# A routed slot's split weights kept in one buffer and remade in a branch where the expert changes

## The chip, the cores and the metric

One Trainium2 chip, one core. The metric is the device time of one execution in microseconds: 819.39 us, the median of three runs (816.16 to 824.21).

## The reference, cut to what matters

Three stages follow each other: a gated recurrent attention, a mixture of experts that sends each token to one of eight, and a feed-forward layer with a cosine in it. The change lies in the second stage and in what the third finds when it begins.

```python
def _moe_ref(x, modality_id, w_gate, modality_bias, w1, w2):   # x 3072x320, w1 8x320x1024, w2 8x1024x320
    logits = x @ w_gate + modality_bias[modality_id]
    e_idx = np.argmax(logits, axis=1)
    ...
    for e in range(E):
        mask = e_idx == e
        h = np.maximum(x[mask] @ w1[e], 0.0)
        out[mask] = gate_w[mask, None] * (h @ w2[e])
    return out

def _moe2_ref(x, w_in, w_out):                                  # w_in 320x2048, w_out 2048x320
    h = x @ w_in
    g = h * np.cos(h)
    return g @ w_out
```

## The kernel before

The tokens of each expert are gathered into slots of 256 rows (`SLOT`). There are twelve such slots (`NS`), in the order of their experts, and up to seven short ones of 128 rows for what is left over (`shorts`). Which expert a slot has is worked out on the chip: `tab0` and `tab` hold each slot's expert and a flag that says whether it differs from that of the slot ahead. `load_w` reads both into registers of SP and issues the loads of the raw weights under the flag: `w1r` and `w2r`, in two halves.

Matmuls run on a split of each operand in two `fp32r` parts, so raw weights must be split before they are used. `split` does it for one f, one of the eight 128-wide pieces of the hidden dimension (`NF`): ACT copies the high parts (`WIH`, line 906, and `WOH`, line 909), and DVE or POOL subtract them from the raw values (line 898, in `sub`): `WIL` and the last rows of `WIH`, and `WOL`. The split weights have two buffers, and slot s uses number s % 2. `prep(n)` makes the split for step n = 8 s + f some steps ahead, for each slot anew, whether the raw weights have changed or not. By the table `VP`, DVE takes the `WIL` part always and the two others at f = 3 and 4; POOL takes the two others at the six other f.

A step of a slot (`bstep(s, f)`, slots 2 to 11) is, in program order: `ffn1` (eight matmuls, line 935), `relu` (ACT line 941, then DVE line 942, into `hh` and `hl`), `ffn2` two steps behind (six matmuls, line 956; its last two steps run in the next slot's f = 0 and 1), one `prep`, and one step of `_decode`. That generator turns the third stage's weights, which lie in memory as 64-bit floats, into 32-bit ones on DVE (lines 1690 to 1707): pieces 3 to 19, each of 5 steps with 6 instructions, loaded by SP into two buffers `raw`. At f = 0 the next slot's rows are gathered (POOL line 828) and `load_w` of the next slot's first half stands; its second half stands at f = 4. At f = 4 to 6 the next slot's rows are transposed and split (`xpose_b`: PE line 848, ACT line 852, DVE line 853). `finish` writes a slot's result (ACT line 971, POOL lines 972 and 962). Every engine works through its own instructions in program order, so DVE's part of a `relu` waits for whatever stands ahead of it on DVE.

Slots 0 and 1 have a loop of their own (line 1306, steps k = 0 to 15), in which DVE also works out the order of the other slots, a chain of small instructions (`plan`, `halves`, `slot_index`, `slot_table`, `out_rows`). There, `prep` is given to POOL altogether for the steps 4 to 9.

The third stage's weights need the same split (`split_c`, sixteen pieces): six pieces stand in slot 11, two in the short slots, and eight in the first tile of the third stage (`c_ffn1`, `c_phase`, `c_cos`, `c_split`, `c_ffn2`). A branch on all engines (line 1540) jumps over the short slots that are not there.

Of the kernel before, what the change touches and what calls it, by code (L numbers as in the profile page):

```python
# [23 lines left out]
DM = H * D  # L24
# [69 lines left out]
def kernel(  # L94
# [816 lines left out]

    VP = ((), (3, 4))

    def prep(n, eng=V):
        s, f = divmod(n, NF)
        if s < NS:
            split(w1r, w2r, f, (s % 2) * NF + f, eng, V if f in VP[bool(s)] else G_)

# [6 lines left out]
    def ffn1(s, f):  # L925
        fs = slice(f * 128, (f + 1) * 128)
        xh, xl = (t_[:, :, (s % 2) * SLOT:(s % 2 + 1) * SLOT] for t_ in (XH, XL))
        ph = hbank(s, f)
        W, Wl = WIH[s % 2][:, :, fs], WIL[s % 2][:, :, fs]
        mms = (  # L930
            (W[:, 0], xh[:, 0]), (Wl[:, 0], xh[:, 0]), (W[:, 1], xh[:, 1]), (Wl[:, 1], xh[:, 1]), (W[:, 2], xh[:, 2]),
            (W[:, 0], xl[:, 0]), (W[:, 1], xl[:, 1]), (W[:, 2], xl[:, 2]),
        )
        for n, (a, x_) in enumerate(mms):
            T_.matmul(out=ph, lhsT=a, rhs=x_, start=(n == 0), stop=(n == len(mms) - 1))  # L935
# [60 lines left out]
    dec, xgs = [iter(())], {}  # L996

# [308 lines left out]
    for k in range(2 * NF):  # L1306
        s, f = divmod(k, NF)
        ffn1(s, f)
        if k == 7:
# [8 lines left out]
        if k == 11:  # L1318
# [191 lines left out]
    qw.close()  # L1510
    qu = ExitStack()
    qu_ = pool(qu, "qu")
    w1u = qu_.tile([128, 3, DF1], F32, name="w1u")
    w2u = qu_.tile([128, NF, DM], F32, name="w2u")
    for a in range(2):
        wu_t[a] += [qu_.tile([128, DM], F32R, name=f"wu{a}{i}") for i in range(2, 4)]
    load_u(1, 0)
    load_u(1, 1)
    xg = xpose_c(0, XS, XH, XL, (2, 3, 2))

    def extra0():
        split_c(6)
        yield
        split_c(7)
        yield
        next(xg)
        yield
        next(xg)
        yield
        next(xg)  # L1530
        yield
# [8 lines left out]
    with ExitStack() as tail:  # L1540
        for u in range(2, NU):
# [89 lines left out]
    for n in range(len(seq) + LAG - 2):  # L1631
# [152 lines left out]
```

## Time and profile before

| | us |
|---|---|
| median of three runs (lowest, highest) | 819.39 (816.16, 824.21) |
| the profiled execution, its own time | 826.95 |
| its span, first to last instruction | 825.2 |
| busy: PE, DVE, ACT, POOL | 735.9, 637.7, 438.3, 340.1 |
| mean granted TensorE clock | 0.947 |

The profile comes from one execution, and its trace is read through views. [...] The timeline gives start, duration, engine, line and operation. The view of groups gives for one kind of instruction the busy time, the mean of one, and how long its engine sat idle just before it. The waits view names who was waited for. L898 is line 898 of the kernel. A duration in the trace can overlap the next instruction's, so the step from one start to the next is what an engine needs for one instruction.

### The profile page before, as it was taken

The page shows a single profiled execution, that of the slowest core. Times are in us where ns is not written, and L with a number is a line of the kernel's source. Part 1 is how long each engine was busy: PE and PEld are TensorE (multiplying, and loading weights), DVE is VectorE, ACT ScalarE, POOL GpSimd, SP SyncE. Part 2 cuts the span into 40 slices and gives each one's busy share as a digit, 9 for nine tenths or more (in the row PEclk, how much of TensorE's full clock was granted, in tenths as well). Part 3 has the DMA queues.
Part 4 walks back from the last instruction along what each step waited for, and adds up shares of the span by engine and source line. Part 5 has one row for each costly group of instructions (what it writes and reads, how often), then busy time and mean ns, then how long its engine had stood idle before and what let it go on. Part 6 is the DMA issues. An engine that isn't in the chain of part 4 may idle for free. (4 is left out here: it accounts for less than half of the span.)

```text
span 825.2 us, 16649 instructions
## 1 busy us (share of the span) xinstructions
PE 735.9 (89%) x5947; PEld 671.1 (81%) x5948; DVE 637.7 (77%) x1320; ACT 438.3 (53%) x1039; POOL 340.1 (41%) x450
## 2 busy tenths in 40 slices
PE   9878988867898889988968899999999999999995
PEld 6777777756887888988858689989899998999995
DVE  6877787779769998999988598767676776666762
ACT  4545555444455555655646466555555555555552
POOL 7646564455587787877875330200200200100201
PEclk6999899989989999989989999999999999999998
DMA  7798787831132282332463201001001000000000
GB/s 180 200 211 226 214 238 219 248 119 41 50 101 62 80 228 70 106 92 68 146 201 105 67 1 33 33 0 33 33 1 33 33 1 1 33 1 0 33 2 33
DMA packets 48650, 73.71 MB, mean 89 GB/s; under 512 B 5518, under 2 KB 33776, under 8 KB 48560
## 3 DMA queue, kind: packets, MB, share of 16 engines
q1 hardware_dynamic: 43808, 59.01, 25.8%
q0 software_dynamic: 3648, 11.82, 4.4%
q10 hardware_dynamic: 1104, 1.75, 0.7%
q8 instruction: 49, 0.80, 0.4%
q14 instruction: 41, 0.34, 0.2%
HBM read 89.82 MB, written 12.22 MB: 124 GB/s over the span
## 5 line engine op out<-in xcount | busy, mean ns | idle before, releaser
L1596 ACT ACTIVATE w1r<-w1r 128x512 f32<-128x512 f32 x96 | 60.7, 632 | 104.2 <-DVE w1r L1591 104.2
L1598 DVE TENSOR_TENSOR w1r<-bk,w1r 128x512 f32<-128x512 f32 x96 | 66.2, 690 | 50.5 <-ACT w1r L1596 49.0
L1589 ACT ACTIVATE w1r<-bk,qtr 128x512 f32<-128x512 f32 x96 | 65.9, 686 | 55.7 <-PE bk L1584 55.7
L935 PE MATMUL bk<-XH,WIH 128*128 128x256 f32 x288 | 81.7, 309 | 15.2 <-POOL WIH L898 5.3
L1590 DVE TENSOR_SCALAR w1r<-w1r 128x512 f32<-128x512 f32 x96 | 41.1, 428 | 51.1 <-ACT w1r L1589 51.0
L941 ACT ACTIVATE hh<-bk 128x256 fp32r<-128x256 f32 x96 | 36.7, 382 | 75.5 <-PE bk L935 75.4
L898 DVE TENSOR_TENSOR WIL<-w1r,WIH 128x256 fp32r<-128x256 f32 x88 | 68.9, 784 | 8.8 <-ACT WIH L906 8.7
L1591 DVE TENSOR_TENSOR w1r<-w1r 128x512 f32<-128x512 f32 x96 | 70.6, 736 | 3.3
L935 PEld LDWEIGHTS bk<-XH,WIH 128*128 128x128 f32 x288 | 58.1, 202 | 18.4 <-POOL WIH L898 6.7
L956 PE MATMUL bk<-WOH,hl 128*128 128x320 f32 x192 | 62.8, 327 | 9.6 <-DVE hl L942 9.6
L1616 PE MATMUL bk<-WOH,gh 128*128 128x320 f32 x228 | 71.0, 312 | 0.0
L1616 PE MATMUL bk<-WOH,gl 128*128 128x320 f32 x228 | 70.6, 310 | 0.0
L1616 PE MATMUL bk<-WOL,gh 128*128 128x320 f32 x228 | 70.5, 309 | 0.0
L898 POOL TENSOR_TENSOR WOL<-w2r,WOH 128x320 fp32r<-128x320 f32 x74 | 67.2, 908 | 0.7 <-ACT WOH L909 0.7
L956 PE MATMUL bk<-WOH,hh 128*128 128x320 f32 x192 | 63.0, 328 | 0.0
L1584 PE MATMUL bk<-XH,WIH 128*128 128x512 f32 x144 | 57.8, 402 | 5.3 <-PEq L1540 4.0
L956 PE MATMUL bk<-WOL,hh 128*128 128x320 f32 x192 | 62.4, 325 | 0.0
L935 PE MATMUL bk<-XL,WIH 128*128 128x256 f32 x288 | 54.6, 298 | 4.5 <-DVE XL L853 4.5
L1584 PE MATMUL bk<-XL,WIH 128*128 128x512 f32 x144 | 57.3, 398 | 0.0
L1584 PE MATMUL bk<-xh,WIH 128*128 128x512 f32 x144 | 56.5, 393 | 0.0
L1584 PE MATMUL bk<-xl,WIH 128*128 128x512 f32 x144 | 56.1, 390 | 0.0
L906 ACT ACTIVATE WIH<-w1r 128x384 fp32r<-128x384 f32 x96 | 49.9, 519 | 9.5 <-DMA w1r<-in_w_dram 9.5
(382 smaller groups left out, 2273.7 us busy)
## 6 DMA issues: line engine op xcount, KB each, us to landing
w2r<-in_w_dram SPq DMA_DIRECT2D x25, 640.0 KB
w1r<-in_w_dram SPq DMA_DIRECT2D x25, 512.0 KB
w1r<-in_w_dram SPq DMA_DIRECT2D x50, 128.0 KB
kvl<-in_kvn_dram SPq DMA_DIRECT2D x12, 484.0 KB
gb<-g_d SPq DMA_DIRECT2D x40, 128.0 KB
raw<-in_w_out_dram SPq DMA_DIRECT2D x8, 640.0 KB
raw<-in_w_in_dram SPq DMA_DIRECT2D x8, 512.0 KB
qkl<-in_qk_dram SPq DMA_DIRECT2D x24, 160.0 KB
```

The lines of the kernel that those rows point to most:

```text
L898: eng.tensor_tensor(out=out_, in0=raw, in1=hi.bitcast(F32), op=ALU.subtract)
L906: A.activation(out=ih, in_=r1[:, :, fs], func=AF.Copy)
L935: T_.matmul(out=ph, lhsT=a, rhs=x_, start=(n == 0), stop=(n == len(mms) - 1))
L941: A.activation(out=hh, in_=ph, func=AF.Relu)
L956: T_.matmul(out=py(s, g), lhsT=a[:, gs], rhs=w_, start=(f == 0 and n == 0), stop=(f == NF - 1 and n == 2),)
L1584: T_.matmul(out=ph, lhsT=a, rhs=x_, start=(n == 0), stop=(n == len(mms) - 1))
L1589: A.activation(out=v, in_=gp[T, f], func=AF.Identity, bias=qtr, scale=1.0 / (2 * math.pi))
L1590: V.tensor_scalar(out=kk, in0=v, scalar1=MAGIC, scalar2=MAGIC, op0=ALU.add, op1=ALU.subtract)
L1591: V.tensor_tensor(out=v, in0=v, in1=kk, op=ALU.subtract)
L1596: A.activation(out=v, in_=v, func=AF.Sin, scale=6.283185)
L1598: V.tensor_tensor(out=g, in0=gp.pop((T, f)), in1=v, op=ALU.mult)
L1616: T_.matmul(out=po, lhsT=a[:, js], rhs=w_, start=(f == 0 and n == 0), stop=(f == NFC - 1 and n == 2),)
```

## The change

Slots no longer have two sets of split weights. All use number 0, and `prep` fills it once, for slot 0. Ahead of each later slot stands `new_weights`: a branch on the flag that `flag_regs` has read into registers of ACT and DVE, and in it the split of all eight f, with every subtraction on DVE. Where the flag is 0, ACT and DVE jump over it. So that the buffer is free there, a slot's last two `ffn2` steps now stand in its own f = 7. Both halves of `load_w(s + 1)` stand at f = 0, behind the branch. `_decode` takes two steps at f = 0 to 4 and one at f = 5 to 7. `split_c` now puts the third stage's pieces 0 to 7 into buffer 1 in slot 10, on ACT and DVE alone, pieces 8 to 11 into buffer 0 in the short slots, and the last four in the third stage's first tile. The second short slot's raw weights go where the third stage's raw weights were.

```diff
-    VP = ((), (3, 4))
-
-    def prep(n, eng=V):
-        s, f = divmod(n, NF)
-        if s < NS:
-            split(w1r, w2r, f, (s % 2) * NF + f, eng, V if f in VP[bool(s)] else G_)
+    def prep(f, eng=V):
+        split(w1r, w2r, f, f, eng)
+
+    def flag_regs(ap):
+        return nc.values_load(ap, engines=(A.engine, V.engine), min_val=0, max_val=1)
+
+    def new_weights(flag):
+
+        with tc.If(flag > 0, preferred_fallthrough_block=False):
+            for f in range(NF):
+                split(w1r, w2r, f, f, V, V)
...
-        W, Wl = WIH[s % 2][:, :, fs], WIL[s % 2][:, :, fs]
+        W, Wl = WIH[0][:, :, fs], WIL[0][:, :, fs]
...
     def bstep(s, f):
+        if f == 0:
+            new_weights(fl.pop(s))
+            load_w(s + 1, 0)
+            gather(s + 1)
+            xgs[s + 1] = xpose_b(s + 1)
         ffn1(s, f)
         relu(s, f)
         if f >= 2:
             ffn2(s, f - 2)
-        elif s > 1:
-            ffn2(s - 1, NF - 2 + f)
-            if f == 1:
-                for g in range(2):
-                    finish(2 * (s - 1) + g, py(s - 1, g))
-        prep(s * NF + f + 3)
-        next(dec[0], None)
         if f == 0:
-            gather(s + 1)
-            xgs[s + 1] = xpose_b(s + 1)
-            load_w(s + 1, 0)
-        if f == 4:
+            for g in range(2):
+                finish(2 * (s - 1) + g, py(s - 1, g))
             load_w(s + 1, 1)
+        for _ in range(2 if f < 5 else 1):
+            next(dec[0], None)
+        if f == 4 and s + 1 < NS:
+            fl[s + 1] = flag_regs(tab[s + 1:s + 2, 1:2])
         if f >= 4:
             next(xgs[s + 1], None)
+        if f == NF - 1:
+            ffn2(s, NF - 2)
+            ffn2(s, NF - 1)
...
     for k in range(2 * NF):
         s, f = divmod(k, NF)
+        if k == NF:
+            new_weights(fl.pop(1))
         ffn1(s, f)
...
-        for n in ((), (2, 3))[k == 3] if k in (2, 3) else (k,) if k < 2 * NF - 1 else ():
-            prep(n + 4, V if n > 5 or n in VK else G_)
+        for n in {0: (4,), 1: (5,), 3: (6, 7)}.get(k, ()):
+            prep(n, G_)
...
+    def cbuf(f):
+        return 1 - f // NF
+
+    def split_c(f, eng=V, eng2=G_):
         if f < 2 * NF:
-            split(w_ir, w_or, f, f, V)
+            split(w_ir, w_or, f, cbuf(f) * NF + f % NF, eng, eng2)
...
     def raw_u(u):
         if u % 2:
-            return w1u, w2u
+            return w_ir[:, :, 0:DF1], w_or[:, 0:NF]
...
-                if f >= 2:
-                    split_c(f - 2)
-    ffn2(NS - 1, NF - 2)
-    ffn2(NS - 1, NF - 1)
+            if s == NS - 2:
+                split_c(f, V, V)
+    for _ in dec[0]:
+        pass
     for g in range(2):
         finish(2 * (NS - 1) + g, py(NS - 1, g))
...
             if T == 0:
-                split_c(NF + f)
+                split_c(NF + 4 + f)
```

On DVE, the end of slot 4 and the start of slot 5, before (`hl` is a `relu`'s second half, `XL` a split row block, `dtu` a decode step, the `WIL`, `WIH` and `WOL` a `prep`):

```order
L853 TENSOR_TENSOR XL<-bk_80,XH 128x256
L942 SCALAR_TENSOR_TENSOR hl_2359<-bk_79,hh_2357 128x256
L898 TENSOR_TENSOR WIL_2534<-w1r,WIH_2532 128x2x128
L1699 SCALAR_TENSOR_TENSOR dtu_3186<-raw_3185,dtu_3186 128x512
L942 SCALAR_TENSOR_TENSOR hl_2358<-bk_78,hh_2356 128x256
L898 TENSOR_TENSOR WIL_2534<-w1r,WIH_2532 128x2x128
L898 TENSOR_TENSOR WIH_2532<-w1r,WIH_2532 64x128
L898 TENSOR_TENSOR WOL_2535<-w2r,WOH_2533 128x320
L1703 TENSOR_SCALAR dtu_3187<-raw_3185 128x512
```

The same place now, with the branch and the first of the eight splits in it:

```order
L853 TENSOR_TENSOR XL<-bk_80,XH 128x256
L947 SCALAR_TENSOR_TENSOR hl_2359<-bk_79,hh_2357 128x256
L1712 SCALAR_TENSOR_TENSOR dtu_3209<-raw_3207,dtu_3209 128x512
L920 COMPARE_AND_BRANCH
L920 UNCONDITIONAL_BRANCH
L898 TENSOR_TENSOR WIL_2354<-w1r,WIH_2352 128x2x128
L898 TENSOR_TENSOR WIH_2352<-w1r,WIH_2352 64x128
L898 TENSOR_TENSOR WOL_2355<-w2r,WOH_2353 128x320
```

A `prep` in every step has become 24 instructions behind a branch, and the decode step stands between the slot's last `hl` and that branch.

On POOL, the first steps of slot 9 before (`XS` is a gather, `ys` and `x_d` a `finish`, `WIH` and `WOL` POOL's part of a `prep`):

```order
L828 DMA XS<-x_d,inv 128x320 x2
L972 COPY ys_3159<-oid 128x1
L962 DMA x_d<-ys_3159,cinv 3072x321
L972 COPY ys_3160<-oid 128x1
L962 DMA x_d<-ys_3160,cinv 3072x321
L898 TENSOR_TENSOR WIH_2532<-w1r,WIH_2532 64x128
L898 TENSOR_TENSOR WOL_2535<-w2r,WOH_2533 128x320
L898 TENSOR_TENSOR WIH_2532<-w1r,WIH_2532 64x128
L898 TENSOR_TENSOR WOL_2535<-w2r,WOH_2533 128x320
```

And all that POOL has in a late slot now:

```order
L828 DMA XS<-x_d,inv 128x320 x2
L977 COPY ys_3179<-oid 128x1
L920 UNCONDITIONAL_BRANCH
L967 DMA x_d<-ys_3179,cinv 3072x321
L977 COPY ys_3180<-oid 128x1
L967 DMA x_d<-ys_3180,cinv 3072x321
```

All of POOL's subtractions have left the slots; its gathers and scatters stay.

## Rows read from the trace of the kernel before

**Rows 1.** The windows view by stage (columns as told under the table above).
```profile
187.00:226.00 39.00, 30.39 (x225) 27.94 (x223) 33.12 (x95) 17.29 (x47) 21.42 (x30) 0.96 0.15 48
...
226.00:430.00 204.00, 171.77 (x1190) 166.35 (x1189) 188.67 (x331) 114.99 (x309) 159.52 (x193) 0.92 0.38 115
...
430.00:459.00 29.00, 22.30 (x163) 21.39 (x162) 18.24 (x37) 16.46 (x45) 13.33 (x18) 0.91 0.28 87
...
484.00:813.00 329.00, 328.78 (x1852) 297.13 (x1851) 232.68 (x390) 180.11 (x307) 25.61 (x29) 1.00 0.05 17
```

**Rows 2.** PE's waits, 226 to 430 us: engine, line, releaser, us, times, longest.
```profile
PE bk L848 <- DVE XL L853: 15.2, 5, 3.5
...
PE bk L935 <- DVE XL L853: 3.4, 4, 1.6
```

**Rows 3.** DVE's timeline: start us, us, engine, line, operation.
```profile
276.90 6.82 DVE L898 TENSOR_TENSOR WIL<-w1r,WIH 128x256 fp32r<-128x256 f32 x1
...
416.70 9.89 DVE L1697 TENSOR_TENSOR dtu<-dtu,dtu 128x640 uint32<-128x640 uint32 x1
```

**Rows 4.** The windows view of two such stalls (columns as in rows 1).
```profile
277.00:283.50 6.50, 4.27 (x32) 3.79 (x30) 6.50 (x1) 3.33 (x10) 6.42 (x11) 1.00 0.08 27
...
194.30:198.10 3.80, 0.00 (x0) 0.00 (x0) 3.80 (x3) 0.00 (x0) 3.80 (x7) 1.00 0.01 2
```

**Rows 5.** Groups by line, 226 to 430 us: count, busy us, mean ns, idle before.
```profile
L898 DVE TENSOR_TENSOR WIL<-w1r,WIH 128x256 fp32r<-128x256 f32 x77 | 62.1, 806 | 6.1 <-ACT WIH L906 5.9
...
L942 DVE SCALAR_TENSOR_TENSOR hl<-bk,hh 128x256 fp32r<-128x256 f32 x81 | 33.2, 410 | 9.2 <-ACT hh L941 9.0
...
L898 POOL TENSOR_TENSOR WOL<-w2r,WOH 128x320 fp32r<-128x320 f32 x57 | 52.4, 919 | 0.0
```

**Rows 6.** DVE's timeline in stretches with little beside it on POOL.
```profile
274.26 0.41 DVE L898 TENSOR_TENSOR WIL<-w1r,WIH 128x256 fp32r<-128x256 f32 x1
274.59 0.67 DVE L1699 SCALAR_TENSOR_TENSOR dtu<-raw,dtu 128x512 uint32<-128x512 uint32 x1
275.19 0.41 DVE L942 SCALAR_TENSOR_TENSOR hl<-bk,hh 128x256 fp32r<-128x256 f32 x1
...
275.86 0.41 DVE L1703 TENSOR_SCALAR dtu<-raw 128x512 uint32<-128x512 uint32 x1
...
411.83 0.81 DVE L1707 SCALAR_TENSOR_TENSOR w_or<-dtu,dtu 128x640 f32<-128x640 f32 x1
```

**Rows 7.** The windows view of one slot, and of the stretch ahead of it.
```profile
288.10:303.40 15.30, 15.30 (x120) 15.12 (x118) 14.54 (x27) 10.74 (x30) 14.25 (x18) 1.00 0.81 230
...
284.70:288.10 3.40, 3.39 (x16) 3.34 (x17) 3.40 (x10) 1.27 (x4) 0.01 (x1) 0.58 0.46 114
```

**Rows 8.** SP's timeline: issues of raw weights under the flag.
```profile
283.75 0.08 SPq L860 DMA_DIRECT2D w1r<-in_w_dram  x1
...
285.09 0.08 SPq L865 DMA_DIRECT2D w2r<-in_w_dram  x1
...
290.82 0.40 SPq L860 DMA_DIRECT2D w1r<-in_w_dram  x1
```

**Rows 9.** The branch on line 1540: DVE's, PE's (ns, at us), SP's wait.
```profile
L1540 DVEq COMPARE_BRANCH  x1: 72/72/72, 454.4 to 454.4; - x1
...
L1540 DVEq EVENT_SEMAPHORE  x1: 21/21/21, 455.0 to 455.0; - x1
...
L1540 PEldq COMPARE_BRANCH  x1: 3912/3912/3912, 454.7 to 454.7; - x1
...
SPq L1540 <- SPq L1540: 6.2, 1, 6.2
```

**Rows 10.** The windows view of the 4 us behind one 640 KB piece's issue (L1673).
```profile
330.30:334.30 4.00, 4.00 (x34) 4.00 (x32) 3.27 (x11) 3.26 (x9) 3.07 (x3) 1.00 0.63 209
```

**Rows 11.** The stall in slot 0: DVE's and PE's timelines.
```profile
190.41 5.85 DVE L1177 TENSOR_SCALAR nT<-nT 128x8 f32<-128x8 f32 x1
...
198.57 0.39 PE L935 MATMUL bk<-XH,WIH 128*128 128x256 f32 x1 [4.86 <-DVE X L1183]
```

More of the change, by code (lines that the diff above doesn't have):

```diff
@@ L950, in ffn2 @@
     def ffn2(s, f):
-        wh, wl = WOH[s % 2][:, f, :], WOL[s % 2][:, f, :]
+        wh, wl = WOH[0][:, f, :], WOL[0][:, f, :]
         hh, hl = hs.pop((s, f))
@@ L979, in bstep @@
             ffn2(s, f - 2)
-        elif s > 1:
-            ffn2(s - 1, NF - 2 + f)
-            if f == 1:
-                for g in range(2):
-                    finish(2 * (s - 1) + g, py(s - 1, g))
-        prep(s * NF + f + 3)
-        next(dec[0], None)
         if f == 0:
-            gather(s + 1)
-            xgs[s + 1] = xpose_b(s + 1)
-            load_w(s + 1, 0)
-        if f == 4:
+            for g in range(2):
+                finish(2 * (s - 1) + g, py(s - 1, g))
             load_w(s + 1, 1)
+        for _ in range(2 if f < 5 else 1):
+            next(dec[0], None)
+        if f == 4 and s + 1 < NS:
+            fl[s + 1] = flag_regs(tab[s + 1:s + 2, 1:2])
         if f >= 4:
             next(xgs[s + 1], None)
-    dec, xgs = [iter(())], {}
+        if f == NF - 1:
+            ffn2(s, NF - 2)
+            ffn2(s, NF - 1)
+    dec, xgs, fl = [iter(())], {}, {}
     wq, wt = [], {}
@@ L1149 @@
     pl_.close()
-    qw = ExitStack()
-    wide(pool(qw, "qw"), 1)
+    wide(pool(ctx, "qw"), 1)
     def small(name, w=E):
@@ L1323 @@
             bg += [slot_table()]
-        if k >= 2:
-            ffn2(*divmod(k - 2, NF))
+        if f >= 2:
+            ffn2(s, f - 2)
+        if f == NF - 1:
+            ffn2(s, NF - 2)
+            ffn2(s, NF - 1)
         if k == 3:
@@ L1356 @@
             next(xgs[1])
+            fl[1] = flag_regs(tab0[:, 2:3])
         if k == 8:
@@ L1378 @@
         run(xgs[k])
+    fl[2] = flag_regs(tab[2:3, 1:2])
     pr.close()
@@ L1393 @@
         G_.memset(t_, 0.0)
-    raw_b = [tb.tile([128, 640, 2], U32, name=f"raw{i}") for i in range(2)]
-    dtu_b = [tb.tile([128, 640], U32, name=f"dtu{i}") for i in range(2)]
+    rb_ = ExitStack()
+    rb = rb_.enter_context(tc.tile_pool(name="rb", bufs=1, side="right", reuse_waits="tile"))
+    raw_b = [rb.tile([128, 640, 2], U32, name=f"raw{i}") for i in range(2)]
+    dtu_b = [rb.tile([128, 640], U32, name=f"dtu{i}") for i in range(2)]
     dec[0] = _decode(nc, (raw_b, dtu_b), w_in, w_out, w_ir, w_or, range(DA, 20))
-    def split_c(f):
+    def cbuf(f):
+        return 1 - f // NF
+    def split_c(f, eng=V, eng2=G_):
         if f < 2 * NF:
-            split(w_ir, w_or, f, f, V)
+            split(w_ir, w_or, f, cbuf(f) * NF + f % NF, eng, eng2)
     def loadx(T, xs):
@@ L1503 @@
                     split_u(0, f - 6)
-                if f >= 2:
-                    split_c(f - 2)
-    ffn2(NS - 1, NF - 2)
-    ffn2(NS - 1, NF - 1)
+            if s == NS - 2:
+                split_c(f, V, V)
+    for _ in dec[0]:
+        pass
     for g in range(2):
         finish(2 * (NS - 1) + g, py(NS - 1, g))
-    qw.close()
+    load_u(1, 0)
+    load_u(1, 1)
+    rb_.close()
     qu = ExitStack()
-    qu_ = pool(qu, "qu")
-    w1u = qu_.tile([128, 3, DF1], F32, name="w1u")
-    w2u = qu_.tile([128, NF, DM], F32, name="w2u")
+    qu_ = pool(qu, "qu", "right")
     for a in range(2):
         wu_t[a] += [qu_.tile([128, DM], F32R, name=f"wu{a}{i}") for i in range(2, 4)]
-    load_u(1, 0)
-    load_u(1, 1)
     xg = xpose_c(0, XS, XH, XL, (2, 3, 2))
     def extra0():
[L1522 to L1531, printed above, removed]
+        for n in range(3):
+            next(xg)
+            yield
+            split_c(NF + n)
+            yield
         xpose_u(1)
         yield
+        split_c(NF + 3)
         yield
@@ L1549 @@
             shorts((u,))
+    qu.close()
     pb.close()
-    qu.close()
     xc = ctx.enter_context(tc.tile_pool(name="xc", bufs=2, reuse_waits="tile"))
-    wide(xc, 1)
     NFC = DF2 // 128
@@ L1573, in c_ffn1 @@
         xh, xl = xh_c[T % 2], xl_c[T % 2]
-        W = WIH[f // NF][:, :, f % NF * 128:(f % NF + 1) * 128]
-        Wl = WIL[f // NF][:, :, f % NF * 128:(f % NF + 1) * 128]
+        W = WIH[cbuf(f)][:, :, f % NF * 128:(f % NF + 1) * 128]
+        Wl = WIL[cbuf(f)][:, :, f % NF * 128:(f % NF + 1) * 128]
         n_ = T * NFC + f
@@ L1613, in c_ffn2 @@
                 gh, gl = gs_[T, f]
-                wh, wl = WOH[f // NF][:, f % NF, :], WOL[f // NF][:, f % NF, :]
+                wh, wl = WOH[cbuf(f)][:, f % NF, :], WOL[cbuf(f)][:, f % NF, :]
                 for n, (a, w_) in enumerate(((gh, wh), (gh, wl), (gl, wh))):
```

## The prediction

> **What bounds the kernel now.** I read the windows view first, by stage [rows 1]. In the third stage, 484 to 813 us, PE is busy 328.78 of 329 us at full clock, and the change takes nothing out of PE's work there. The routed slots 2 to 11 lie at 226 to 430 us: there PE is busy 171.77 of 204 us at a clock of 0.92, while DVE is busy 188.67. So PE waits for DVE in this stage, and the waits view says where: five groups of PE's waits, from 15.2 us for `XL` down to 3.4 us [rows 2], fill the 32.2 us that PE is idle.
>
> DVE's own sum is swollen. One 128x256 subtraction stands there for 6.82 us and one decode instruction for 9.89 us [rows 3]; the same kinds take 0.41 and 0.81 us where POOL has little to do [rows 6]. In the windows of two such stalls DVE holds one or a few instructions while POOL is busy without a gap, 6.42 of 6.50 us and 3.80 of 3.80 us, and they end when POOL's run of subtractions ends [rows 4]. The mean of the `WIL` subtraction over the stage is 806 ns, that of `hl`, whose one input is in PSUM, 410 ns [rows 5]. What DVE suffers from is POOL's share of `prep`, of which the `WOL` part alone is 52.4 us in these slots [rows 5].
>
> Against that stands one slot that ran well: 288.1 to 303.4 us, 120 matmuls, PE busy throughout at a clock of 1.00, 15.30 us [rows 7]. That is PE's own need for a slot with its three transposes. [...]
>
> **How often the branch is taken.** SP's timeline answers it from before: an issue of `load_w` under a flag of 0 takes 0.08 us, one under a flag of 1 takes 0.40 us [rows 8]. Among the loads for slots 2 to 11 only one slot's pair, that for slot 6, has the long form. So of eleven branches one is taken.
>
> **The change part by part.**
>
> *Slots 2 to 11.* Removed: nine preps of ten on ACT and DVE, all of them on POOL. With POOL down to four indirect DMAs and two small copies per slot, DVE's instructions take their short form. DVE's need per slot is then worked out from the steps between starts in [rows 6]: a 128x256 instruction 0.33 us, a 128x512 one with two inputs 0.60; one with a single input is as long as the 128x256 one, 0.41, and needs the same 0.33. Eight `hl` and three `XL`: 11 x 0.33 = 3.6 us. Thirteen decode steps are 2.6 pieces; a piece of 512 has three instructions of each kind, 2.8 us, one of 640 (0.81 us long, about 0.74 from start to start) some 3.4: 7.3 to 8.9 us. The register load and branch I put at 1.2. Together 12.1 to 13.7 us, under PE's 15.3: the bound goes from DVE to PE. ACT, busy 115 of 204 us [rows 1], is relieved too.
>
> PE needs 10 x 15.3 = 153 us. To that comes what I expect PE to lose:
> (a) The seam. The next `ffn1` waits until ACT and DVE have gone past the branch. Behind its last `ffn1` PE still has three `ffn2` of about 0.9 us (half of a step's 1.9), 2.7 us. In that time `relu` takes about 1.1 (0.41 for `hl`, the same on ACT, and the hops), a decode step up to 0.7, the branch 0.6 (454.4 to 455.0 on DVE for the jump on line 1540 [rows 9]). So they fit, with 0.3 us to spare, and the bank of f = 0 is late by a few tenths: 0.7 us per seam, 7 us. Bounds: nothing, and 4 us per seam (a rival).
> (b) Raw pieces. A 640 KB piece takes about 4 us from its issue until the DMA engines have moved it [rows 10], and DVE now goes through a piece in 2.5 steps, 4.6 us, where it had 9 to 10. Behind the branch SP has eight conditional issues ahead of the next piece, 3.6 us (four take 1.4 from first to last [rows 8]). A piece that falls there comes 1 to 2 us late: 0.5 us per slot over seven slots, 3.5 us; bounds 0 and 20 us (a rival).
> (c) Slot 6. Its 2.9 MB, (384 + 320) x 1024 values of 4 bytes, are issued at the start of slot 5, with decode's pieces behind them in SP's order. Slot 5 offers 15.3 us; the window of the old load moved 230 GB/s on average [rows 7], which gives 12.6 us. It fits, but the pieces come late: 4 us. Then the eight splits, on DVE 0.33, 0.40 (128x320, in proportion) and less than 0.33: 1.0 us per f, which stays ahead of PE's 1.9 once the first is there: 2.5 us more. Bounds 2 and 12.
> (d) Jumps that stall as PE's did on line 1540, 3.9 us [rows 9]: half of one, 2 us in all; bounds 0 and 40 (rival 1). [...]
> Two `ffn2` steps of slot 1 leave this stage, 1.8 us that only change place. So 204 - 1.8 becomes 153 + 7 + 3.5 + 6.5 + 2 = 172, and the gain is 30 us; with ends of 48 (no loss at all) and 8.
>
> *Slots 0 and 1, 187 to 226 us.* The 0.1 us instruction on line 1177 takes 5.85 us, and PE then waits 4.86 us [rows 11]. POOL's run beside it holds the preps 6 to 9, and the last two, 194.3 to 198.1, belong to slot 1 [rows 4]. They go: 3.8 us. The other idle of this stage (39 - 30.39 - 4.86 = 3.7 us) has the same cause further on; I take 3.2 of it, and for the wait at the new seam and the gather of slot 2 give nothing back. Gain 7, bounds 3.8 and 10.
>
> *Short slots, 430 to 459 us.* No decode is left there, four `split_c` with POOL's part come in. PE is idle 6.7 of 29 us at a clock of 0.91 [rows 1]; 3.9 of it is PE's own jump [rows 9], which stays. Gain 2.5, bounds 0 and 5. Eight `split_c` in slot 10 cost DVE 8 us in a slot without decode: 3.6 + 1.2 + 8 = 12.8, under PE's 15.3, so nothing. The first tile of the third stage loses four splits: gain 1.
>
> **The sum** is 30 + 7 + 2.5 + 1 = 40.5 us of the profiled 826.95 (span 825.2), so 786. The runs' median lies 7.6 us below the profiled execution; 819.4 - 40.5 = 779, which I forecast.
>
> **The rivals.**
> 1. *The jumps stall on every seam* (slower). If ACT's or DVE's jump costs 3.9 us as PE's did, then each of eleven seams loses 3.9 - 0.3 = 3.6 us and about 1.5 us of low clock behind it: 56 us instead of the 9 of (a) and (d). That is 47 more than forecast, 826 us, slower than before by 7; with SP's 6.2 us per jump, 851. It decides from about 3.5 us a jump. For it speaks PE's row; against it DVE's, 0.6 us for the same line [rows 9]. [...]
> 2. *Decode becomes the bound.* If raw pieces come late by 1.3 us each, all sixteen, on DVE ahead of an `hl`, PE loses 20 us: 799. For it: 4.6 us per piece against a 4 us load behind SP's conditional issues. Against: two buffers, and no wait for a raw piece among PE's now.
> 3. *Everything fits*: (a) to (d) cost 4 us instead of 19, and slots 0 and 1 give their 10: 761.
> 4. *It doesn't do what it says*: the flag is set at many seams. Each then costs what (c) says, 6.5 us less one seam's 0.7: 5.8 more at ten seams, 58, and ACT and DVE gain little: 825 or more. Against it speak [rows 8].
>
> **How the numbers follow.** The forecast's case (770 to 790) has 0.5, rival 3 0.18, rival 2 with other partial losses (790 to 808) 0.24, rival 1 0.05, rival 4 0.03; of the last two 0.05 end slower, 0.03 within 1%. The range leaves out the last two and the end of rival 3: 756 to 804. A measurement here can tell about 1%, 8 us. Faster by more than that: 0.92; within it 0.03; slower 0.05.
>
> **What would show it right or wrong.** Right: in the new profile no DVE instruction of the slots over 2 us, `WIL` gone from nine seams, POOL busy under 80 us between slots 2 and 11, PE over 90% busy there, and slots about 16.5 us apart. Term (b) shows as DVE's waits for `raw`, (c) as a longer seam at slot 6, (d) as branch rows of several us. It is wrong if DVE's long instructions stay without POOL's subtractions, if PE's waits at the seams exceed 2 us each, or if the third stage's 329 us change.

## The result, and the profile after

Run side by side, the kernel before took 818.21 us (median of four runs) and the changed one 788.74: a ratio of 0.963, with a 95% interval of 0.957 to 0.969. That is 29.5 us less, in the range and of the forecast sign, but 10 us short of the 779 forecast.

The profiled executions last 825.2 us (before) and 787.8 us (after) by their spans, 37.4 apart, and stage by stage this can be taken to pieces. Slot 0 begins at 170.8 us before and at 166.6 after. Ahead of it both compute the same, and in the twelve further profiles of this study slot 0 starts between 165.1 and 169.3 us (at 165.8 in a second profile of the kernel before), so I count these 4.2 us as scatter. The windows view of the kernel before, cut where the slots really begin and end (slots 0 and 1, slots 2 to 11, the short slots), has the columns of [rows 1]: start and end of a stretch, its length, then for each of PE, PE's weight loads, DVE, ACT and POOL the busy time with the number of instructions in brackets, the granted TensorE clock as a share of full speed, the share of time in which the DMA engines were busy, and GB/s:

```profile
170.80:226.00 55.20, 41.21 (x310) 37.63 (x308) 48.83 (x147) 24.64 (x67) 30.88 (x45) 0.91 0.21 67
...
226.00:430.40 204.40, 172.17 (x1192) 166.75 (x1191) 188.87 (x331) 115.22 (x309) 159.52 (x193) 0.92 0.38 115
...
430.40:458.80 28.40, 21.70 (x161) 20.79 (x160) 18.04 (x36) 16.23 (x44) 13.33 (x18) 0.92 0.29 88
```

The same view of the changed kernel, with the third stage as its last row:

```profile
166.60:216.30 49.70, 41.19 (x320) 38.69 (x318) 36.81 (x136) 17.34 (x48) 17.66 (x26) 0.93 0.20 62
...
216.30:396.00 179.70, 162.22 (x1178) 158.71 (x1179) 112.20 (x259) 62.62 (x172) 54.58 (x66) 0.95 0.41 125
...
396.00:422.10 26.10, 20.53 (x161) 19.38 (x160) 16.56 (x31) 16.89 (x49) 15.66 (x22) 1.00 0.50 153
...
422.10:787.80 365.70, 355.64 (x1980) 319.88 (x1980) 248.91 (x415) 192.37 (x328) 32.89 (x37) 0.99 0.06 21
```

Slots 0 and 1 went from 55.2 to 49.7 us, and the two `ffn2` steps of 1.8 us (the prediction's estimate) that came into them are to be added: 7.3 us gained. Slots 2 to 11 went from 204.4 to 179.7: 24.7, of which 1.8 only moved, so 22.9. The short slots gained 2.3 and the third stage 0.7 (366.4, from 458.8 to the end, against 365.7). The change itself is worth 33.2 us in these two executions, with a scatter of about a microsecond in a stage: in the second profile of the kernel before, slots 0 and 1 took 54.2 us. DVE's busy time in slots 2 to 11 fell from 188.87 to 112.20 us, POOL's from 159.52 to 54.58, and PE's share of the stage rose from 84% to 90%.

The view of groups of the changed kernel in slots 2 to 11 (line, engine, operation, tiles, count, busy us, mean ns, idle before) answers to [rows 3, 5]:

```profile
L947 DVE SCALAR_TENSOR_TENSOR hl<-bk,hh 128x256 fp32r<-128x256 f32 x80 | 33.6, 420 | 44.0 <-ACT hh L946 40.4 <-ACTq L920 3.4
...
L1710 DVE TENSOR_TENSOR dtu<-dtu,dtu 128x512 uint32<-128x512 uint32 x9 | 6.2, 685 | 0.1
...
L1710 DVE TENSOR_TENSOR dtu<-dtu,dtu 128x640 uint32<-128x640 uint32 x8 | 6.6, 820 | 0.1
...
L967 POOL DMA_INDIRECT x_d<-ys,cinv x22 | 25.6, 1164 | 115.7 <-ACT hh L946 97.8 <-ACT WIH L906 10.2 <-ACTq L920 4.3
...
L828 POOL DMA_INDIRECT XS<-x_d,inv x18 | 20.4, 1133 | 5.4 <-issue 4.8 <-PE bk L940 0.6
```

The decode instruction in the second and third of these rows reads so in the kernel before, 226 to 430 us:

```profile
L1697 DVE TENSOR_TENSOR dtu<-dtu,dtu 128x512 uint32<-128x512 uint32 x9 | 13.6, 1506 | 0.0
...
L1697 DVE TENSOR_TENSOR dtu<-dtu,dtu 128x640 uint32<-128x640 uint32 x7 | 14.8, 2107 | 0.0
```

Its means were 1506 and 2107 ns there, and single ones stood for up to 9.89 us. Now they are 685 and 820, and no DVE instruction in these slots takes over 1 us. POOL has its indirect DMAs and copies left, and `hl` costs what it did.

Where PE still loses time is told by the starts of slots 0 to 11, taken as the first matmul of each slot's first `ffn1` in PE's timeline. Each entry is the time from one start to the next, in us:

| slot | 0 | 1 | 2 | 3 | 4 | 5 | 6 | 7 | 8 | 9 | 10 |
|---|---|---|---|---|---|---|---|---|---|---|---|
| before | 31.7 | 23.5 | 20.7 | 21.0 | 20.5 | 18.2 | 19.0 | 16.2 | 22.5 | 20.7 | 17.2 |
| after | 29.1 | 20.6 | 23.1 | 15.6 | 16.8 | 24.3 | 22.0 | 15.9 | 15.5 | 15.6 | 15.8 |

Five slots, called clean from here on, take 15.5 to 15.9 us: PE's own need of 15.3 [rows 7] and a seam (the passage from one slot to the next) of 0.2 to 0.6. Slots 2, 5 and 6 take 22.6 us more than three of 15.6. The waits views name the reason: PE waits for `hl`, and once for ACT at the branch; DVE waits for decode's raw pieces, and SP at the branch (engine, line, releaser, us, times, longest; PE's from slot 0 on):

```profile
PE bk L940 <- DVE hl L947: 17.5, 5, 6.6
...
PE bk L940 <- ACTq L920: 1.5, 1, 1.5
...
DVE dtu L1703 <- DMA raw<-in_w_out_dram: 8.2, 1, 8.2
...
DVE dtu L1703 <- DMA raw<-in_w_in_dram: 7.5, 2, 5.4
...
SPq L860 <- DVEq L920: 3.7, 1, 3.7
```

The timelines show the two places (start us, us, engine, line, operation; in brackets the idle time and its releaser). At slot 2 the first raw piece is late, and at slot 5 SP issues slot 6's 2.9 MB first and a raw piece behind them:

```profile
223.88 0.43 DVE L1703 TENSOR_SCALAR dtu<-raw 128x512 uint32<-128x512 uint32 x1 [5.40 <-DMA raw<-in_w_in_dram]
...
225.02 0.58 PE L940 MATMUL bk<-XH,WIH 128*128 128x256 f32 x1 [4.41 <-DVE hl L947]
...
270.99 0.40 SPq L860 DMA_DIRECT2D w1r<-in_w_dram  x1
...
278.45 1.18 SPq L1686 DMA_DIRECT2D raw<-in_w_out_dram  x2
...
287.13 0.49 DVE L1703 TENSOR_SCALAR dtu<-raw 128x640 uint32<-128x640 uint32 x1 [8.21 <-DMA raw<-in_w_out_dram]
...
288.42 0.58 PE L940 MATMUL bk<-XH,WIH 128*128 128x256 f32 x1 [6.58 <-DVE hl L947]
```

DVE stands at the decode instruction for 5.40 and 8.21 us, and `hl`, which PE needs, is queued behind it. PE then waits 4.41 and 6.58 us.

The third place is slot 6, where the branch is taken. DVE's and PE's timelines:

```profile
295.21 0.42 DVE L898 TENSOR_TENSOR WIL<-w1r,WIH 128x256 fp32r<-128x256 f32 x1
...
295.55 0.28 DVE L898 TENSOR_TENSOR WIH<-w1r,WIH 64x128 fp32r<-64x128 f32 x1
...
295.75 0.48 DVE L898 TENSOR_TENSOR WOL<-w2r,WOH 128x320 fp32r<-128x320 f32 x1
...
302.33 0.47 DVE L898 TENSOR_TENSOR WOL<-w2r,WOH 128x320 fp32r<-128x320 f32 x1
...
302.73 0.41 DVE L947 SCALAR_TENSOR_TENSOR hl<-bk,hh 128x256 fp32r<-128x256 f32 x1
...
303.19 0.58 PE L940 MATMUL bk<-XH,WIH 128*128 128x256 f32 x1 [5.11 <-DVE hl L947]
```

DVE goes through 24 subtractions from 295.21 to 302.73 us, and only then comes `hl` of f = 0. PE has run `ffn1` of f = 0 and 1 and waits 5.11 us. A single record of the branch is short. The view of line 920 (ns least/median/most, first and last start):

```profile
L920 ACTq COMPARE_BRANCH  x21: 38/39/55, 191.9 to 379.7; - x21
...
L920 DVEq COMPARE_BRANCH  x21: 43/47/63, 194.0 to 380.6; - x21
```

These are two records at each of the ten seams where the block is jumped over and one where it is run, 38 to 63 ns each. To pass the branch takes longer than a record: from the first of a pair to the second, with a semaphore event between them, 0.2 to 1.5 us go by. At slot 2, ACT's pair runs from 215.5 to 216.3 us, and PE's first matmul of the slot starts at 216.32 after waiting 1.5 us for it.

### The profile page after: what moved, and what is told of

It reads as the page before. It is cut to its first block, busy times and chain, and to the rows that moved or that the text cites. A ratio compares the mean times of both kernels' runs of the same rounds, so it can differ in the third digit from the quotient of the medians.

```text
span 787.8 us, 16155 instructions
## 1 busy us (share of the span) xinstructions
PE 723.5 (92%) x5947; PEld 661.8 (84%) x5948; DVE 542.0 (69%) x1230; ACT 376.3 (48%) x879; POOL 218.6 (28%) x300
## 5 line engine op out<-in xcount | busy, mean ns | idle before, releaser
L940 PE MATMUL bk<-XH,WIH 128*128 128x256 f32 x288 | 80.8, 308 | 20.6 <-DVE hl L947 17.5
L947 DVE SCALAR_TENSOR_TENSOR hl<-bk,hh 128x256 fp32r<-128x256 f32 x96 | 40.3, 420 | 50.9 <-ACT hh L946 47.2
L1604 DVE TENSOR_TENSOR w1r<-w1r 128x512 f32<-128x512 f32 x96 | 68.2, 711 | 3.3
L961 PE MATMUL bk<-WOH,hl 128*128 128x320 f32 x192 | 60.9, 317 | 5.3 <-DVE hl L947 5.3
L967 POOL DMA_INDIRECT x_d<-ys,cinv x26 | 29.6, 1140 | 128.3 <-ACT hh L946 97.8
L961 PE MATMUL bk<-WOH,hh 128*128 128x320 f32 x192 | 61.0, 318 | 0.0
L961 PE MATMUL bk<-WOL,hh 128*128 128x320 f32 x192 | 60.5, 315 | 0.0
L940 PE MATMUL bk<-XH,WIL 128*128 128x256 f32 x192 | 51.8, 291 | 0.0
L940 PE MATMUL bk<-XL,WIH 128*128 128x256 f32 x288 | 51.6, 289 | 0.0
```

The costliest lines, as they stand in the source:

```text
L947: V.scalar_tensor_tensor(out=hl, in0=ph, scalar=0.0, in1=hh.bitcast(F32), op0=ALU.max, op1=ALU.subtract)
L961: T_.matmul(out=py(s, g), lhsT=a[:, gs], rhs=w_, start=(f == 0 and n == 0), stop=(f == NF - 1 and n == 2),)
L967: r = G_.indirect_dma_start(out=dst, out_offset=bass.IndirectOffsetOnAxis(ap=idx, axis=0), in_=src, in_offset=None, bounds_check=NTOK - 1, ...
L1604: V.tensor_tensor(out=v, in0=v, in1=kk, op=ALU.subtract)
```

## The experiments

Twelve kernels were run. Times are medians of four runs where a ratio to the kernel before, measured beside them, is given, and of one run otherwise. Slot times are read as in the table above.

**1. POOL's hold on DVE, from the side of the kernel before.** All splits stay, but from slot 2 on POOL's subtractions go to DVE.

```diff
-  split(w1r, w2r, f, (s % 2) * NF + f, eng, V if f in VP[bool(s)] else G_)
+  split(w1r, w2r, f, (s % 2) * NF + f, eng, V if s > 1 or f in VP[bool(s)] else G_)
```

> The kernel before, with all its splits, but for slots 2 and later POOL's subtractions are done on DVE: DVE gets about 130 more instructions there, POOL none. Theory (POOL's subtractions starve DVE; without them a slot costs DVE 3.6 for hl and XL, 4.7 for eight decode steps and 7.5 for 24 subtractions, 15.8 us, against PE's 15.3): no DVE instruction over 2 us in slots 2 to 11, slots near 16.5 to 17.5 us where they took 20.4, 780 to 795 us. Rival (DVE has too much work, POOL relieves it): the added 0.6 us per split, 7.5 us less what it had, makes slots longer, 825 to 850.

Measured: 788.38 us, ratio 0.965 (0.957 to 0.973), as fast as the whole change. Slots 2 to 10 took 18.1, 15.2, 15.6, 15.9, 16.5, 16.3, 16.3, 16.5, 16.6 us. The groups on DVE in slots 2 to 11:

```profile
L898 DVE TENSOR_TENSOR WOL<-w2r,WOH 128x320 fp32r<-128x320 f32 x77 | 36.9, 479 | 1.0 <-issue 1.0
...
L942 DVE SCALAR_TENSOR_TENSOR hl<-bk,hh 128x256 fp32r<-128x256 f32 x79 | 32.4, 411 | 1.9 <-ACT hh L941 1.9
...
L898 DVE TENSOR_TENSOR WIL<-w1r,WIH 128x256 fp32r<-128x256 f32 x77 | 31.6, 411 | 1.7 <-ACT WIH L906 1.7
...
L1697 DVE TENSOR_TENSOR dtu<-dtu,dtu 128x640 uint32<-128x640 uint32 x7 | 5.7, 814 | 0.0
```

DVE does 57 more `WOL` subtractions than before, and yet its instructions are short: `WIL` 411 ns where it had 806 [rows 5], the decode instruction 814 where it had 2107. So it was not the amount of work that made the slots long, but POOL's subtractions beside DVE. (5.3 us of PE's waits before were for POOL's own `WIH`; this run takes these away as well, run 2 has the hold alone.) The slots here are even shorter than those of the changed kernel. The total is the same because as much is lost around them: slots 0 and 1 take 53.7 us, in the changed kernel 49.7, and from the start of slot 11 to the third stage 53.6 us pass, in the changed kernel 41.3. Decode, at 8 steps per slot, ends there only at 405 us, and third-stage splits stand there that the changed kernel has in slot 10; how much of it each costs was not tried.

**2. POOL's hold, put back.** In the changed kernel POOL gets subtractions whose results nobody reads, at six of eight steps in slots 2 to 10.

```diff
         hs[s, f] = (hh, hl)
+        if 2 <= s < NS - 1 and f not in (3, 4):
+            for _ in range(2):
+                sub(G_, wu_t[0][0][:, 0:256], hh.bitcast(F32), hl)
```

> The changed kernel with work added that nothing reads: in slots 2 to 10, at six of eight steps, POOL subtracts hl from hh twice (128x256) into a buffer that is free there, so that POOL has again about the subtractions per step that it had in the kernel before. Theory (POOL's subtractions hold up DVE's instructions whose inputs lie in SBUF): decode's instructions, 0.4 to 0.8 us alone, show means well over 1 us and single ones of several us, PE waits for hl and XL again, slots near 18 to 20 us, 805 to 830 us. Rival (what counted was DVE's own work, less now): DVE's means stay, 787 to 792 us.

Measured: 809.86 us in one run, 21 more than the changed kernel. But the waits view has ACT waiting 34.2 us for POOL to have read `hh`, a side effect of this edit, so it doesn't settle the matter. The next run has `sub(G_, wu_t[0][0], xs_u[0][:, 0:DM], xs_u[1][:, 0:DM])` in that place:

> As in the run before with added POOL work, but free of its side effect (there ACT waited 34.2 us for POOL to have read hh): in slots 2 to 10, at six of eight steps, POOL subtracts twice between two buffers of zeros (128x320) that no other engine writes or reads there. Nothing waits for these, and they need only the order on POOL. Theory (the contention alone holds DVE's instructions with inputs in SBUF up): DVE's decode instructions beside POOL's runs stand for several us, slots 2 to 8 take 17 to 21 us apart from the waits they have in the changed kernel, and slot 9, which has no decode, stays near 15.6: 800 to 825 us. Rival (the earlier run was slower for ACT's wait for POOL): 787 to 793.

Measured: 811.9 us in one run, 23 more than the changed kernel. No engine waits for POOL's added subtractions themselves, but the gathers that stand behind them on POOL come later, and PE waits for their rows in slots 5, 9 and 10 (first line below). In slots 3, 4, 7 and 8 PE waits for `hl` and `XL` alone: they took 17.5, 18.5, 19.5, 17.4 us in place of 15.6, 16.8, 15.9, 15.5. Slot 9, without decode, took 16.6, with 0.84 of it a wait for a gather, and slot 10, whose third-stage splits are DVE's, 19.1 in place of 15.8. PE's wait and DVE's groups, 215 to 405 us:

```profile
PE bk L848 <- DMA XS<-x_d,inv: 5.0, 4, 2.0
...
L947 DVE SCALAR_TENSOR_TENSOR hl<-bk,hh 128x256 fp32r<-128x256 f32 x74 | 30.7, 415 | 27.5 <-ACT hh L946 25.9 <-ACTq L920 1.5
...
L853 DVE TENSOR_TENSOR XL<-bk,XH 128x256 fp32r<-128x256 f32 x29 | 11.9, 415 | 7.6 <-ACT XH L852 7.6
...
L1713 DVE TENSOR_TENSOR dtu<-dtu,dtu 128x640 uint32<-128x640 uint32 x8 | 8.8, 1095 | 0.1
...
L1719 DVE TENSOR_SCALAR dtu<-raw 128x512 uint32<-128x512 uint32 x9 | 8.1, 899 | 0.0
```

`hl` and `XL`, which have one input in PSUM, stay at 415 ns. The two decode instructions, all of whose inputs lie in SBUF, grew from 820 to 1095 and from 419 to 899. That is POOL's hold alone, without any wait for a result; about 5 of the 23 us are PE's waits for the late gathers. One thing expected did not come: no single instruction stood over 2.3 us, where in the kernel before it was up to 9.9. The length of POOL's runs is not the reason: ten of the added subtractions stand back to back for 10.66 us, from 251.29 us on, while in the kernel before a DVE instruction was held 6.82 us beside a run of 11 instructions, 7.85 us in all. The runs don't show why POOL's other mix of subtractions holds DVE so much longer.

**3. Only leave the work out.** The kernel before, with splits for slots 0, 1, 6 and 7 alone; the two buffers still hold the right weights for the rest.

```diff
-        if s < NS:
+        if s in (0, 1, 6, 7):
```

> The kernel before with its two buffers and its order, but the splits left out for slots 2 to 5 and 8 to 11, whose expert is that of the slot two before (the buffers still hold its weights). Theory (the change's gain is the removed splits, and its new order costs it the waits at slots 2, 5 and 6, some 20 us): slots 2 to 11 take 160 to 168 us, 770 to 778 in all, faster than the changed kernel. Rival (the gain needs the new order of decode and seams): 785 to 800.

Measured: 782.31 us, ratio 0.956 (0.948 to 0.963): 6 us under the changed kernel by the medians, with intervals that overlap, and between the two expectations. The slots came as the theory had them. The windows view from the start of slot 2 to 373.6 us, 15.2 us behind the start of slot 11:

```profile
218.10:373.60 155.50, 151.73 (x1165) 150.08 (x1163) 113.27 (x225) 69.00 (x183) 80.35 (x99) 1.00 0.46 141
```

Slots 3 to 5 and 8 to 10 took 15.2 us each, slot 6 16.9 and slot 7, for which the other buffer is filled, 16.2: splits spread over the steps of the slots cost 1.0 to 1.7 us where the block in the branch cost 6.4. What was missed is the end: with 8 decode steps per slot, 34.7 us pass from 373.6 to the third stage, in the changed kernel 26.1 from the end of slot 11.

**4. The branch taken away.** The changed kernel with the eight splits written at slot 6's seam and nothing at the others; the flags' registers are gone, and `flag` is the slot's number.

```diff
-        with tc.If(flag > 0, preferred_fallthrough_block=False):
+        if flag == 6:
```

> The changed kernel without a branch and without its flag registers: the eight splits stand in the program at the seam of slot 6 alone, where this input needs them, and nothing stands at the other ten. Theory (the jumps are hidden: clean slots of the changed kernel take 15.5 to 15.9 us and the seam at 255 us shows PE without a wait): 786 to 789 us, the same as the changed kernel, the waits at slots 2, 5 and 6 stay. Rival (each seam pays for its branch, about 0.5 us, and 1.5 at slot 2): 781 to 784.

Measured: 778.26 us, ratio 0.948 (0.941 to 0.956): 10.5 us less than the changed kernel by the medians, a larger gain than the rival had. Clean slots took 15.6 to 15.8, as with the branch, so the jump on ACT and DVE is hidden there. The gain lies at slots 1 (18.8, was 20.6), 2 (17.8, was 23.1), 4 (15.6, was 16.8) and 5 (22.7, was 24.3). SP's, DVE's and PE's timelines at slot 2:

```profile
212.92 0.07 SPq L860 DMA_DIRECT2D w1r<-in_w_dram  x1
...
220.07 0.86 DVE L1703 TENSOR_SCALAR dtu<-raw 128x512 uint32<-128x512 uint32 x1 [1.97 <-DMA raw<-in_w_in_dram]
...
221.66 0.39 PE L940 MATMUL bk<-XH,WIH 128*128 128x256 f32 x1 [1.42 <-DVE hl L947]
```

SP issues slot 3's loads at 212.92, 2.6 us ahead of slot 2's start. In the changed kernel it waited 3.7 us for DVE to pass the branch, since the branch may still read the raw weights that the load overwrites, and the raw piece stands behind these loads. DVE's wait for the piece is 1.97 here and was 5.40. So the branch costs mainly through SP: 8.1 us at slots 2, 4 and 5. The 1.8 us at slot 1 are another matter: up to the last `ffn2` of that slot both kernels take the same time, and then PE waits 1.5 us for ACT's branch, a wait that is gone here.

**5. The splits at every seam.** The same edit without the condition.

> The changed kernel without a branch, with the eight splits done at all eleven seams. Theory (a block of 24 subtractions, 7.5 us on DVE, stands ahead of the next hl and cost slot 6 some 6.4 us): every one of the ten other seams loses 5 to 6.5 us, 840 to 855 us, slower than before. Rival (slot 6 was long for its late loads, not for the block): under 810.

Measured: 851.15 us in one run. Slots 3 to 10 took 21.4 to 27.1 us; slot 6, at 22.2, is now no longer than the others. In the six slots that are clean in run 4 (3, 4 and 7 to 10) the block of splits costs 5.6 to 7.6 us, and remaking the weights at every seam would have made the kernel slower than before.

**6. The loads moved.** The changed kernel, one branch, but the next slot's loads, both at f = 0 before, stand behind decode's steps at f = 1 and 5.

```diff
-            load_w(s + 1, 0)
...
-            load_w(s + 1, 1)
...
+        if f == 1:
+            load_w(s + 1, 0)
+        if f == 5:
+            load_w(s + 1, 1)
```

> The changed kernel with one thing moved: the loads of the next slot's raw weights are issued behind decode's at f = 1 and f = 5 in place of twice at f = 0. The branch stays one. Theory (what the changed kernel loses at slots 2 and 5 is SP standing at the branch with the raw piece behind it, and the piece queued behind 2.9 MB): slot 2 near 16.5 and slot 5 near 17, with 5 to 6 us more at slot 6, whose second half comes later: 776 to 782 us. Rival (the four-part branch was what shortened these slots): 785 to 790.

Measured: 776.3 us, ratio 0.943 (0.936 to 0.950). Slot 2 took 16.9, slot 4 15.5, slot 5 15.6; slot 6 24.9, as its data come later. PE's two waits in slot 6:

```profile
282.90 0.38 PE L940 MATMUL bk<-XH,WIL 128*128 128x256 f32 x1 [1.85 <-DVE WIL L898]
...
290.43 0.58 PE L940 MATMUL bk<-XH,WIH 128*128 128x256 f32 x1 [4.92 <-DVE hl L947]
```

The place of two lines gave 12 us by the medians. The late raw pieces were a matter of SP's order.

**7. Decode spread.** The changed kernel, decode from f = 4 of slot 2 on, then 11 steps per slot; loads unchanged.

```diff
-        for _ in range(2 if f < 5 else 1):
+        for _ in range((1, 0, 0, 0, 2, 2, 2, 2)[f] if s == 2 else (2, 1, 1, 2, 1, 1, 2, 1)[f]):
```

> The changed kernel with decode spread: in slot 2 it starts at f = 4, and then does 11 steps per slot in place of 13 (slots 3 to 9). Loads and branch as in the changed kernel. Theory (the late raw pieces at slots 2, 4 and 5 cost 7.5, 1.2 and 8.7 us): slot 2 near 16.5, slot 4 near 15.7, slot 5 near 20, 776 to 781 us. Rival (DVE waits for raw there, but PE's loss has another cause, the branch): 786 to 790.

Measured: 786.68 us, ratio 0.958 (0.953 to 0.964): a miss, in the rival's range. But the rival's reason does not hold, as PE's wait still follows DVE's wait for a piece: slot 2 fell to 18.2 and slot 4 to 15.5, but slot 5 rose to 27.5. SP's, DVE's and PE's timelines there:

```profile
273.05 0.51 SPq L1681 DMA_DIRECT2D raw<-in_w_in_dram  x1
...
285.17 0.43 DVE L1703 TENSOR_SCALAR dtu<-raw 128x512 uint32<-128x512 uint32 x1 [11.29 <-DMA raw<-in_w_in_dram]
...
286.31 0.58 PE L940 MATMUL bk<-XH,WIH 128*128 128x256 f32 x1 [8.95 <-DVE hl L947]
```

The raw piece is still issued behind slot 6's load, and DVE reached it earlier: it waits 11.29 us instead of 8.21. Fewer steps don't help against an order of issues.

**8. The branch in four parts**, two f each, at the seam and behind `relu` of f = 0, 2 and 4, with the loads at f = 1 and 5 (those for slot 2 move within slot 1, from its f = 3 and 4 to f = 5).

```diff
-            for f in range(NF):
+            for f in (2 * j, 2 * j + 1):
                 split(w1r, w2r, f, f, V, V)
...
+        if f in (0, 2, 4):
+            new_weights(fl[s], f // 2 + 1)
```

> The changed kernel with its branch cut in four (two pieces f each): the first at the seam, the others after relu of f = 0, 2 and 4, and the loads of the next slot's raw weights behind them (at f = 1 and 5). Decode as in the changed kernel. Theory (slot 6 loses 6.4 us because hl stands behind 24 subtractions, and raw pieces come late because SP waits at the branch and puts them behind the load): slot 6 near 17 us, slot 2's wait for raw 2 us or less, 774 to 780 us. Rival (a branch costs by itself, 33 more of them on each of two engines): 788 to 795.

Measured: 780.89 us, ratio 0.953 (0.948 to 0.957), 4.6 more than run 6 with its one branch, with intervals that just overlap. Slot 6 took 24.2, not 17: its first weights came late (PE waited 3.16 us for the `WIL` of f = 0), and later chunks brought waits of 1.2 to 1.5. Other slots took up to 0.9 us more than in run 6.

**9. All together**: 7 and 8, and the subtractions of the preps of f = 3 to 7 of slot 0 on DVE.

```diff
-            prep(n, G_)
+            split(w1r, w2r, n, n, V, V)
```

> The four-part branch and the spread decode together, and the POOL subtractions of the preps of f = 3 to 7 of slot 0 on DVE. Theory: slots 2 to 10 all within 15.4 to 17 us, and slots 0 and 1 shorter by 4 to 8 us as no DVE instruction there stands 2 to 4 us beside POOL: 762 to 770 us. Rival (the parts overlap, DVE has too much in slot 0): 774 to 780.

Measured: 772.07 us, ratio 0.942 (0.937 to 0.947), the lowest median here, 47 us under the kernel before and 17 under the changed one, but above the expected range. Slot 0 took 26.1, slot 6 18.6. Slot 2 still took 18.0 and clean slots 15.7 to 16.4, where four branches may cost their share; that was not tried alone. Against run 6, with one edit, the intervals overlap.

**10. The kernel before, with DVE in slots 0 and 1 too.** All subtractions from f = 3 of slot 0 on are DVE's.

> The kernel before with all its splits, its two buffers and its order, but all subtractions of the preps from f = 3 of slot 0 on are done on DVE, those in slots 0 and 1 too. Theory (POOL holds DVE up for 2 to 4 us at a time in slots 0 and 1 as well: with its subtractions gone slot 0 took 26.1 instead of 29 to 30 us in the last run): 778 to 785 us, 4 to 8 under the kernel that moves them from slot 2 on alone. Rival (DVE is too full in slots 0 and 1 to take eleven more splits): 788 to 796.

Measured: 783.16 us, ratio 0.952 (0.945 to 0.958). Slot 0 took 25.5 us, in run 1 31.1. So it is in slot 0, too, that POOL's subtractions hold DVE up. The changed kernel keeps the subtractions of five preps on POOL there. DVE's and POOL's timelines of it:

```profile
185.69 3.95 DVE L1184 TENSOR_SCALAR nT<-nT 128x8 f32<-128x8 f32 x1
...
189.56 0.16 DVE L667 TENSOR_SCALAR hF<-rk 128x4 f32<-128x4 f32 x1
...
185.68 0.75 POOL L898 TENSOR_TENSOR WIL<-w1r,WIH 128x256 fp32r<-128x256 f32 x1
...
186.39 0.46 POOL L898 TENSOR_TENSOR WIH<-w1r,WIH 64x128 fp32r<-64x128 f32 x1
...
188.77 0.85 POOL L898 TENSOR_TENSOR WOL<-w2r,WOH 128x320 fp32r<-128x320 f32 x1
```

A `TENSOR_SCALAR` on 128x8 numbers, which takes 0.15 us in run 10 (line 1177 there), stands from 185.69 for 3.95 us, which is just POOL's run of six subtractions, 185.68 to 189.62.

**11. The kernel before once more**, for its scatter.

> The kernel before once more, unchanged, for a second profile. Theory (its long DVE instructions beside POOL come in every execution, and 4 us of its first profile are scatter ahead of slot 0): slot 0 starts near 166 us in place of 170.8, slots 2 to 11 take 198 to 205 us, with DVE instructions over 3 us in them. Rival (the first profile was an outlier in these slots): under 195 us.

Measured: 823.28 us, span 821.6. Slot 0 starts at 165.8 and slots 2 to 11 take 205.2 us, against 204.4. The same instructions stand long in both profiles (6.81 and 9.90 us here, 6.82 and 9.89 in [rows 3]). The stalls belong to the program's order, not to one execution.

## Why the prediction was right, and where its sizes were off

**What bounds the kernel.** Right. That DVE was the bound in slots 2 to 11, and by POOL's subtractions more than by its own work, is shown from both sides: taken from POOL they free DVE even where it has to do them itself (run 1), and put back they stretch DVE's decode instructions but not `hl` or `XL` (run 2). That PE waited for DVE alone was not quite right: of the waits in [rows 2]'s view 5.3 us were for POOL's `WIH`. Run 2 shows which instructions the hold reached: those with a PSUM input stay at 415 ns, one with two inputs in SBUF goes from 820 to 1095 and one with a single input there from 419 to 899. By what POOL holds DVE up was not shown.

**DVE's need per slot**, put at 12.1 to 13.7 us against PE's 15.3: about right. In two clean slots DVE is busy 11.65 and 13.29 us (239.4 to 255.0 and 318.0 to 333.9); the register load and branch, put at 1.2 without a row behind it, are not counted as busy there.

**How often the branch is taken.** Right: ACT and DVE have one more record of line 920 than twice the ten seams at which it was not taken, so it was taken once of eleven.

**(a) and (d), the seam and the jumps, put at 7 and 2.** (d) is nothing: no record of the branch took over 63 ns, passing it took 1.5 us at most where rival 1 needed 3.5, and clean slots are as long with the branch as without (run 4). Rival 1 falls with it. The 1.5 us of low clock that it adds to each seam are an estimate from [rows 7]: the stretch of 3.40 us at 0.58 held one step, 15.3 / 8 = 1.9 us at a clock of 1.00. The changed kernel doesn't show them behind a branch: after the 1.5 us for ACT at slot 2 the clock was 1.00 (216.3 to 219.0 us), and 0.50 (225.0 to 228.9) after the 4.41 us for `hl`. Clean seams cost 0.2 to 0.6 us, a little under the forecast. Only at slot 2 did PE stand for the branch itself, 1.5 us for ACT. But most of what the branch costs was sought in the wrong place. The step that looked at who waits behind it took ACT, DVE and PE, and reckoned with SP only for its conditional issues. SP waits for DVE to pass, 3.7 us at slot 2, and raw pieces stand behind. By run 4 the branch costs 10.5 us in all: 1.8 at the end of slot 1, and nearly all the rest under (b) and (c).

**(b), raw pieces, 3.5 us over seven slots.** Mis-sized: 7.5 us at slot 2 (23.1 less 15.6) and 1.2 at slot 4, 8.7, and nothing at the others. A piece did come late behind eight conditional issues, but only where SP had first stood at the branch and no earlier piece lay ready: the first one, at slot 2.

**(c), slot 6, 4 and 2.5 us.** Mis-sized in both parts, and one step of it was false. The late piece cost 8.7 us at slot 5. The splits cost 6.4, because "stays ahead of PE's 1.9 once the first is there" took f by f what stands in the program as one block: 24 subtractions ahead of the first `hl`, 7.5 us by DVE's timeline. Run 5 shows the same price at other seams, and run 3 shows 1.7 us for spread splits.

**The sum.** For slots 2 to 11 it was 153 + 7 + 3.5 + 6.5 + 2 = 172. Measured: 153 + 3 (ten seams of 0.3) + 8.7 + 15.1 + 0 = 179.8, against 179.7 from the windows view. The other terms came out: slots 0 and 1 7.3 (forecast 7), short slots 2.3 (2.5), third stage 0.7 (1). So 33.2 us in the profiled pair against 40.5. (b) and (c) cost 13.8 us more than forecast, and (a) and (d) 6 less; that the gap is 7 us and not 14 is luck, as errors of opposite sign cancelled. (The gain with no loss at all, given as 48, comes to 49 by its own terms.) Between the medians it is 29.5, with an interval from 25 to 35 us that holds 33.2 and not 40.5.

**Rival 2**, decode as the bound, was right about the place (raw pieces, DVE, `hl`) and wrong about the number: three late pieces, for which DVE waited 5.4, 2.1 and 8.2 us, not sixteen with 1.3. Rival 3 was the state that the slots reach without the branch and the block (run 3). Rival 4's price is measured by run 5, 851 us where 825 or more was said. Of the signs named ahead, the short DVE instructions, POOL's 54.58 us, PE's 90% and the unchanged third stage came; slots 16.5 us apart did not: they are 18.0 apart on average.

## What to carry to other kernels

When an engine's instructions have long outliers, look at what the other engines do in just these microseconds before counting work: here moving POOL's subtractions onto the busy DVE itself gained 3.5% (run 1). A branch or a wait is to be priced on the engine that issues loads, too, with all loads queued behind it, and a block of work in a branch by what its engine has queued behind the whole block. One load placed behind a small urgent one, not ahead of it, was worth 12 us.

## What the runs showed of the hardware that was not expected

The hold seems to work in the other direction as well. In run 1 DVE works almost without a gap and POOL's timeline has, at the one place where it still subtracts:

```profile
379.56 5.15 POOL L898 TENSOR_TENSOR WIH<-w_ir,WIH 64x128 fp32r<-64x128 f32 x1
```

The same shape takes POOL 0.46 us in the run of six shown at 10. POOL's 22 scatter DMAs are longer in run 1 as well: nine of them take 2.1 to 2.9 us, and their mean is 1.66, in the changed kernel 1.16; its small copies have a mean of 0.89 us, there 0.26. No run tried this direction by itself. And a stall does not need a large instruction: in the changed kernel one on 128x8 numbers stood 3.95 us, through the whole of POOL's run of six subtractions (185.68 to 189.62 us).
